# Gated linear attention with a routed expert layer: f loaded one chunk ahead of q, k and v, and the work that needs f alone done one step sooner

## Chip, cores, metric

One core of one Trainium2 chip. The metric is the time of one execution on the device in microseconds; a run is profiled once and timed in several rounds beside the kernel before.

## The reference, cut to what matters

A gated linear attention (batch 4, 8 heads, 768 positions, head size 48) feeds a layer of eight experts. The change touches the attention alone; the experts' routing and matrices (some 304 us of the span) are the same in both kernels.

```python
def _attn_ref(q, k, v, f_logit):
    f = 1.0 / (1.0 + np.exp(-f_logit))
    state = np.zeros((B, H, D, D))
    for t in range(S):
        state = f[:, :, t, :, None] * state + np.einsum('bhd,bhe->bhde', k[:, :, t], v[:, :, t])
        y[:, :, t] = np.einsum('bhd,bhde->bhe', q[:, :, t], state)
    return y
# then: assign each token to one of 8 experts by logits = x @ w_gate (384 tokens each),
# out = relu(x @ w1[e]) @ w2[e]
```

## The kernel before: the parts that matter

The attention runs in 24 chunks of 128 positions (4 batches x 6). A chunk passes through stages, and step s works on several chunks at once: a part listed with stage n works on chunk s - n. PE, VectorE (DVE), ScalarE (ACT) and GpSimd (POOL) keep the order of these lists; the loads on SyncE (SP) do not have to. The names: g is minus the logarithm of the forget factors, L its cumulative sum; dl is L within limits; eq and ek are its two exponentials; qg = q * eq and kg = k * ek; T is their transpose in PSUM, qT and kT the copies; A are the scores, am the masked ones; Y is the output in PSUM, x its copy, X and xT the transpose of x; R is the old state times its decay gl; "ends" are the sums from which gl comes.

```python
    def load(G):                      # four loads of 192 KB, rows of 192 bytes
        for nm, src in (("f", f_logit), ("q", q), ("k", k), ("v", v)):
            t = work.tile([128, H, DH], FP32, name=nm, tag=nm, bufs={"f": 3, "q": 4, "k": 4, "v": 7}[nm])
            nc.sync.dma_start(...)
    def clamp(G):  # POOL   f
    def decays(G): # ACT    f <- exp(-f), g <- ln(1 + f)
    def split(G):  # DVE upper <- g; POOL low <- g - upper     (chunks 2 and later)
    def split_high(G): # ACT high <- upper
    def sums(G):   # PE     L <- cumulative sums of g (two matmuls: high, low)
        if G["i"] == STAGES - 1:      # STAGES = 6
            idle_turns(3, ps("nothing", "sum"))
    def factors(G):# DVE dl <- L; ACT eq <- exp(-dl), ek <- exp(dl)
    def gated_q(G):# DVE    qg <- q * eq
    def gated_k(G):# POOL   kg <- k * ek
    def span(G):   # DVE spans <- ends; POOL gl; ACT gl
    def columns(G, nm, t):            # PE transposes qg, kg; 4 idle turns each for chunks 1, 2
    def queries(G):# PE Y += R qT; ACT x <- Y; store of x issued by ACT
    # ... transposed: PE X <- x; x_copy: DVE xT <- X; gate: PE; scores: PE A, DVE am; values: PE Y

    FIRST = ((decayed, 2), (q_columns, 2), (k_columns, 2), (transposed, 5), (sums, 1))
    FILLING = (FIRST + ((x_copy, 5), (factors, 1), (k_copy, 2), (added, 2), (values, 4), (halves, 1), (gate, 5),
                        (gated_q, 1), (new_state, 2), (decays, 0), (gated_k, 1), (span, 1), (to_logits, 5),
                        (split, 0), (beside, 0), (clamp, -1), (queries, 4), (split_high, 0), (scores, 3)))
    FULL = ((decayed, 2), (decays, 0), (transposed, 5), (sums, 1), (added, 2), (x_copy, 5), (factors, 1),
            (split, 0), (split_high, 0), (k_copy, 3), (halves, 1), (new_state, 2), (values, 4), (span, 1),
            (gate, 5), (gated_q, 1), (gated_k, 1), (to_logits, 5), (q_columns, 2), (k_columns, 2), ...,
            (beside, 0), (clamp, -1), (queries, 4), (scores, 3))
    # ... FILLING for steps 0 to 5, FULL to step 25, LAST to step 28;
    # `beside` holds small pieces of the routing, on VectorE and GpSimd

    constants()
    idle_turns(19, ps("nothing", "sum"))   # matmuls on constants that keep PE's clock up
    clamp(chunks[0])
    attention(0, 2)
    idle_turns(12, ps("nothing", "sum"))
    attention(2, 3)
    nc.vector.memset(a_bufs[2][:], 0.0)
```

Of the kernel before, what the change touches and what calls it, by code (L numbers as in the profile page):

```python
# [26 lines left out]
def kernel(  # L27
# [60 lines left out]
    def ps(name, tag="bank"):  # L88
        return banks.tile([128, 512], FP32, name=name, tag=tag, bufs=BANKS[tag])
# [34 lines left out]
    def idle_turns(n, nothing):  # L124

        for _ in range(n):
            nc.tensor.matmul(out=nothing[:, 0:CAP], lhsT=ones[:], rhs=idle[:], start=True,  # L127
                             stop=True)
# [28 lines left out]

    state, spare = {}, {}

    def load(G):  # L160
        b, c = G["b"], G["c"]
        for nm, src in (("f", f_logit), ("q", q), ("k", k), ("v", v)):

            t = work.tile([128, H, DH], FP32, name=nm, tag=nm,
                          bufs={"f": 3, "q": 4, "k": 4, "v": 7}[nm])
            nc.sync.dma_start(
                out=t[:], in_=src[b, :, C * c:C * c + C, :].rearrange("h t d -> t h d"))
            G[nm] = t

    def clamp(G):  # L170
        f = G["f"]
        nc.gpsimd.tensor_scalar(out=f[:], in0=f[:], scalar1=3.0e38, scalar2=-40.0,
                                op0=ALU.min, op1=ALU.max)
# [23 lines left out]

    def sums(G):
        g = g_bufs[G["i"] % NB]
        if G["i"] == STAGES - 1:  # L200

            idle_turns(3, ps("nothing", "sum"))
        G["L"] = L = ps("L")
        Lv = L[:, 0:D].rearrange("t (h d) -> t h d", d=DH)
        if "terms" in G:
            for n, term in enumerate(G["terms"]):
                nc.tensor.matmul(out=L[:, 0:D], lhsT=wcum_r[:],
                                 rhs=term[:].rearrange("t h d -> t (h d)"),
                                 start=(n == 0), stop=(n == 1))
        else:  # L210
            nc.tensor.matmul(out=Lv, lhsT=wcum[:], rhs=g[:, :, 0:DH], start=True, stop=True)
# [176 lines left out]
    chunks = [{"b": b, "c": c, "i": c * B + b} for c in range(NCH) for b in range(B)]  # L388
    AHEAD = 2
    STAGES = 6  # L390

    def beside(G):
# [6 lines left out]



    FIRST = ((decayed, 2), (q_columns, 2), (k_columns, 2), (transposed, 5), (sums, 1))
    FILLING = (FIRST + ((x_copy, 5), (factors, 1), (k_copy, 2),
                        (added, 2), (values, 4), (halves, 1), (gate, 5), (gated_q, 1),
                        (new_state, 2), (decays, 0), (gated_k, 1), (span, 1), (to_logits, 5),
                        (split, 0), (beside, 0), (clamp, -1), (queries, 4), (split_high, 0),
                        (scores, 3)))
    FULL = ((decayed, 2), (decays, 0), (transposed, 5), (sums, 1), (added, 2), (x_copy, 5),
            (factors, 1), (split, 0), (split_high, 0), (k_copy, 3), (halves, 1), (new_state, 2),
            (values, 4), (span, 1), (gate, 5), (gated_q, 1), (gated_k, 1), (to_logits, 5),  # L410
            (q_columns, 2), (k_columns, 2), (k_last, 2), (beside, 0), (clamp, -1), (queries, 4),
            (scores, 3))
    LAST = ((scores, 3),) + FIRST + ((x_copy, 5), (k_copy, 2), (values, 4), (queries, 4),
                                     (counts_so_far, 5), (gate, 5), (to_logits, 5),
# [3 lines left out]

    def attention(first, last):
        for step in range(first, last):  # L420
            if step + AHEAD < len(chunks):
                load(chunks[step + AHEAD])
            for part, stage in (FILLING if step < STAGES else
                                FULL if step < len(chunks) + 2 else LAST):
                if 0 <= step - stage < len(chunks):
                    part(chunks[step - stage])
                if part is sums and small_pe:
                    small_pe.popleft()()
                if part is beside:
                    for _ in range(min(len(small), 1 if step >= len(chunks) + 2 else 2)):  # L430
                        small.popleft()()

    for G in chunks[0:AHEAD]:
        load(G)
    nc.sync.dma_start(out=wg[:], in_=moe_w_gate.rearrange("(c p) e -> p c e", p=128))
    ENG = mybir.EngineType
    in_order = tc.manual_schedule(engines={ENG.PE, ENG.DVE, ENG.Activation, ENG.Pool})
# [1 line left out]
    constants()  # L439
    idle_turns(19, ps("nothing", "sum"))  # L440
    clamp(chunks[0])
    attention(0, 2)
    idle_turns(12, ps("nothing", "sum"))
    attention(2, 3)
    nc.vector.memset(a_bufs[2][:], 0.0)
    nc.scalar.dma_start(out=xd[N:N + 32, :], in_=zeros[:])
# [251 lines left out]
    def assign_and_run(begun=None, also=None, again=None, exact=None):  # L698
# [158 lines left out]
        def assign_exact(choice, over, pick, slots):  # L857
# [9 lines left out]
            n = E * NT  # L867
            sums = P[:, 0:n].rearrange("p (e c) -> p e c", c=NT)
            nc.tensor.matmul(out=sums, lhsT=ones[:], rhs=by_e(tie), start=True, stop=True)
            nc.tensor.matmul(out=P[:, n:2 * n], lhsT=after[:], rhs=by_e(tie), start=True, stop=True)  # L870
            sure = rt([NT, E], "sure", BF16)
# [285 lines left out]
        stack.close()  # L1157

    attention(3, ALL - 13)
    assert not small  # L1160
    begun, part, at_steps = begin()
# [109 lines left out]
    with tc.If(again[0] > 0):  # L1271
# [9 lines left out]
        with tc.For_i(0, B, 1) as b:  # L1281
# [7 lines left out]
            for c in range(NCH):  # L1289
                G = {"x": x[:, c, :]}  # L1290
# [42 lines left out]
```

## Time and profile before

| | before |
|---|---|
| time (median of 4) | 459.16 us (458.33 to 461.3) |
| profiled span | 457.7 us |
| first L (L(0)) starts | 6.86 us |
| L of step 6, of step 7, of step 23 | 30.80, 36.85, 129.79 us |
| last logits of the attention | 153.94 us |
| last logits to the end (routing and experts) | 303.8 us |

L(i), the cumulative sum of chunk i, is one matmul group a step, so its starts are a good clock. Before, step s has L(s-1); after the change, L(s). So one compares by step number. The page, the stretches and one step are shown in the prediction.

### The profile page before, as it was taken

What the parts mean: (1) busy time and instruction counts of PE and PEld (TensorE: products, weight loads), DVE (VectorE), ACT (ScalarE), POOL (GpSimd) and SP (SyncE); (2) the same over time, 40 slices, a digit from 0 to 9 for tenths busy, and PEclk for the clock granted to TensorE, in tenths of its full rate; (3) what the DMA queues carried; (4) which work ended last, traced back from release to release, by engine and by line L of the source; (5) the groups of instructions that cost most, each with busy time, mean ns of one, the idle gap of its engine ahead of it and who ended that gap; (6) DMA issues with size and microseconds to landing.
All of it is one profiled execution on the core that took longest, in us unless ns stands there. A gap on an engine that the chain in (4) does not pass through costs nothing. (4 is left out here: it accounts for less than half of the span.)

```text
span 457.7 us, 11902 instructions
## 1 busy us (share of the span) xinstructions
PE 437.1 (96%) x4893; PEld 293.8 (64%) x4893; DVE 266.0 (58%) x878; ACT 138.8 (30%) x322; POOL 135.6 (30%) x189
## 2 busy tenths in 40 slices
PE   8999999999999669999999999999999999999994
PEld 5788888888888535565565565565565565556552
DVE  5779986778987686657547547647637636000000
ACT  4566665565552001202202212212212212212210
POOL 1556655555551021032032033033023025101001
PEclk9999999999999859999999999999999999999998
DMA  9999988978611127082082082072082087400001
GB/s 158 186 196 196 201 177 190 202 166 189 141 37 39 36 86 245 1 310 70 8 299 74 8 292 80 3 290 82 6 292 70 17 292 243 174 19 34 0 19 39
DMA packets 118399, 59.11 MB, mean 129 GB/s; under 512 B 101664, under 2 KB 112960, under 8 KB 118336
## 3 DMA queue, kind: packets, MB, share of 16 engines
q1 hardware_dynamic: 111760, 44.06, 38.4%
q0 software_dynamic: 3072, 9.44, 6.3%
q10 hardware_dynamic: 3504, 4.77, 3.0%
q8 instruction: 40, 0.66, 0.6%
q14 instruction: 23, 0.19, 0.1%
HBM read 48.77 MB, written 9.49 MB: 127 GB/s over the span
## 5 line engine op out<-in xcount | busy, mean ns | idle before, releaser
L1054 PE MATMUL H<-xeT,w 128*128 128x384 f32 x384 | 132.6, 496 | 0.1
L1054 PEld LDWEIGHTS H<-xeT,w 128*128 128x128 f32 x384 | 69.1, 190 | 45.7 <-issue 4.0
L1066 PE MATMUL O<-w,hT 128*128 128x384 f32 x192 | 67.0, 491 | 0.0
L1066 PE MATMUL last_O<-w,hT 128*128 128x384 f32 x192 | 66.7, 491 | 0.0
L1058 ACT ACTIVATE hT<-H 128x384 f32<-128x384 f32 x64 | 31.4, 491 | 101.3 <-PE H L1054 85.3
L1066 PEld LDWEIGHTS last_O<-w,hT 128*128 128x128 f32 x192 | 35.1, 190 | 22.8 <-issue 1.9
L1066 PEld LDWEIGHTS O<-w,hT 128*128 128x128 f32 x192 | 34.9, 190 | 21.5 <-issue 1.3
L1071 POOL DMA_INDIRECT out_dram<-o,token x21 | 21.2, 1012 | 83.6 <-ACT o L1070 83.3
L324 DVE COPY_PREDICATED am<-mask,A 128x512 f32<-128x512 int32 x48 | 32.3, 726 | 14.9 <-PE A L319 14.9
L971 POOL TENSOR_TENSOR block<-past 128x72 f32<-128x72 f32 x8 | 2.4, 300 | 111.8 <-DVE at L551 100.1
L190 POOL TENSOR_TENSOR low<-g,upper 128x384 fp32r<-128x384 f32 x22 | 22.3, 1013 | 43.8 <-DVE upper L188 37.8
L1046 ACT COPY xeT<-Xe 128x384 f32<-128x384 f32 x24 | 11.4, 479 | 58.0 <-PE Xe L1043 57.7
L334 PE MATMUL Y<-v,am 128*64 128x48 f32 x768 | 27.6, 223 | 0.9 <-DVE am L324 0.9
L319 PE MATMUL A<-qT,kT 48*64 48x128 f32 x768 | 26.3, 272 | 0.0
L334 PEld LDWEIGHTS Y<-v,am 128*64 128x64 f32 x768 | 24.8, 138 | 1.9 <-DVE am L324 1.4
L1013 POOL DMA_INDIRECT xe<-xd,token x21 | 21.4, 1021 | 10.9 <-issue 4.3
L243 POOL TENSOR_TENSOR kg<-k,ek 128x384 f32<-128x384 f32 x23 | 23.1, 1004 | 2.4 <-ACT ek L221 2.4
L319 PEld LDWEIGHTS A<-qT,kT 48*64 48x64 f32 x768 | 21.2, 133 | 0.6 <-issue 0.6
L127 PE MATMUL nothing<-idle,ones 128*128 128x384 bf16 x74 | 19.8, 407 | 1.6 <-DVE ones L132 1.5
L220 ACT ACTIVATE eq<-dl 128x384 f32<-128x384 f32 x24 | 12.5, 522 | 24.7 <-DVE dl L218 24.7
L1070 ACT COPY o<-O 128x384 f32<-128x384 f32 x12 | 5.8, 479 | 40.7 <-PE O L1066 40.7
L237 DVE TENSOR_TENSOR qg<-q,eq 128x384 f32<-128x384 f32 x24 | 17.4, 725 | 0.6 <-ACT eq L220 0.6
(223 smaller groups left out, 659.7 us busy)
## 6 DMA issues: line engine op xcount, KB each, us to landing
w<-in_moe_w_dram SPq DMA_DIRECT2D x16, 1536.0 KB, 7.4
f<-in_f_logit_dram SPq DMA_DIRECT2D x24, 192.0 KB, 5.0
q<-in_q_dram SPq DMA_DIRECT2D x24, 192.0 KB, 4.8
k<-in_k_dram SPq DMA_DIRECT2D x24, 192.0 KB, 5.2
v<-in_v_dram SPq DMA_DIRECT2D x24, 192.0 KB, 5.2
xd<-x ACTq DMA_DIRECT2D x24, 192.0 KB, 3.4
xe<-xd,token POOLq DMA_INDIRECT x21, 3.1
out_dram<-o,token POOLq DMA_INDIRECT x21, 2.6
```

The costliest lines, as they stand in the source:

```text
L127: nc.tensor.matmul(out=nothing[:, 0:CAP], lhsT=ones[:], rhs=idle[:], start=True, stop=True)
L190: nc.gpsimd.tensor_tensor(out=low[:], in0=g[:, :, 0:DH], in1=upper[:].bitcast(FP32), op=ALU.subtract)
L237: nc.vector.tensor_tensor(out=G["qg"][:, :, 0:DH], in0=G["q"][:], in1=G["eq"][:], op=ALU.mult)
L243: engine.tensor_tensor(out=G["kg"][:, :, 0:DH], in0=G["k"][:], in1=G["ek"][:], op=ALU.mult)
L319: nc.tensor.matmul(out=A[par][HC * j:HC * j + HC, 128 * hp:128 * hp + 128], lhsT=G["kT"][rows, hp, HC * j:HC * j + HC], rhs=G["qT"][rows, ...
L324: nc.vector.copy_predicated(am[:, par], mask[:].unsqueeze(1).to_broadcast((128, HP, 128)), A[par][:].rearrange("s (a t) -> s a t", t=128))
L334: nc.tensor.matmul(out=Y[par][HC * j:HC * j + HC, DH * hp:DH * hp + DH], lhsT=G["am"][:, par, hp, HC * j:HC * j + HC], rhs=G["v"][:, 2 * h ...
L1013: nc.gpsimd.indirect_dma_start(out=xe[:], out_offset=None, in_=xd[:, :], in_offset=bass.IndirectOffsetOnAxis(ap=token[:, i:i + 1], axis=0))
L1054: nc.tensor.matmul(out=L["H"][:, 0:CAP], lhsT=L["w1"][:, d, 128 * ft:128 * ft + 128], rhs=xT[:, d, :], start=(d == 0), stop=(d == DC - 1))
L1058: nc.scalar.activation(out=hT[:, ft, :], in_=L["H"][:, 0:CAP], func=AF.Relu)
L1066: nc.tensor.matmul(out=L["O"][:, 0:D], lhsT=hT[:, ft, 128 * i:128 * i + 128], rhs=L["w2"][:, ft, :], start=(ft == 0), stop=(ft == FC - 1))
L1071: nc.gpsimd.indirect_dma_start(out=outs[next(tiles)][:, :], out_offset=bass.IndirectOffsetOnAxis(ap=L["token"][:, i:i + 1], axis=0), in_=o ...
```

## The change

Intent: f is the head of the longest chain (clamp, exp, ln, split, L, dl, eq, then qg). Load it earlier and do all of that chain one step sooner, so that q and k meet factors that have long been ready.

```diff
-    def load(G):
+    def load(G, names):
...
     def sums(G):
-        if G["i"] == STAGES - 1:
-            idle_turns(3, ps("nothing", "sum"))
...
-    FIRST = (... (sums, 1))
+    FIRST = (... (sums, 0))
     FILLING: (factors, 1) (halves, 1) (span, 1) -> 0;  (decays, 0) (split, 0) (split_high, 0) -> -1;  (clamp, -1) -> -2
              (gated_q, 1) and (gated_k, 1) move up, to stand right after (x_copy, 5), ahead of factors
     FULL:    the same stages, the same move of gated_q and gated_k
...
-            if step + AHEAD < len(chunks):
-                load(chunks[step + AHEAD])
+            for ahead, names in (AHEAD + 1, "f"), (AHEAD, "qkv"):
+                if AHEAD <= step + ahead < len(chunks) and (ahead == AHEAD or step >= 0):
+                    load(chunks[step + ahead], names)
...
-    for G in chunks[0:AHEAD]:
-        load(G)
+    for n, names in (0, "f"), (1, "f"), (0, "qk"), (2, "f"), (0, "v"), (1, "qkv"):
+        load(chunks[n], names)
...
-    attention(0, 2)
+    attention(-1, 2)
```

(The lines on the lists are told, not quoted.)

More of the change, by code (lines that the diff above doesn't have):

```diff
@@ L158 @@
     state, spare = {}, {}
-    def load(G):
+    def load(G, names):
         b, c = G["b"], G["c"]
-        for nm, src in (("f", f_logit), ("q", q), ("k", k), ("v", v)):
+        for nm in names:
+            src = {"f": f_logit, "q": q, "k": k, "v": v}[nm]
             t = work.tile([128, H, DH], FP32, name=nm, tag=nm,
@@ L395 @@
     ALL = len(chunks) + STAGES - 1
-    FIRST = ((decayed, 2), (q_columns, 2), (k_columns, 2), (transposed, 5), (sums, 1))
-    FILLING = (FIRST + ((x_copy, 5), (factors, 1), (k_copy, 2),
-                        (added, 2), (values, 4), (halves, 1), (gate, 5), (gated_q, 1),
-                        (new_state, 2), (decays, 0), (gated_k, 1), (span, 1), (to_logits, 5),
-                        (split, 0), (beside, 0), (clamp, -1), (queries, 4), (split_high, 0),
+    FIRST = ((decayed, 2), (q_columns, 2), (k_columns, 2), (transposed, 5), (sums, 0))
+    FILLING = (FIRST + ((x_copy, 5), (gated_q, 1), (gated_k, 1), (factors, 0), (k_copy, 2),
+                        (added, 2), (values, 4), (halves, 0), (gate, 5),
+                        (new_state, 2), (decays, -1), (span, 0), (to_logits, 5),
+                        (split, -1), (beside, 0), (clamp, -2), (queries, 4), (split_high, -1),
                         (scores, 3)))
-    FULL = ((decayed, 2), (decays, 0), (transposed, 5), (sums, 1), (added, 2), (x_copy, 5),
-            (factors, 1), (split, 0), (split_high, 0), (k_copy, 3), (halves, 1), (new_state, 2),
-            (values, 4), (span, 1), (gate, 5), (gated_q, 1), (gated_k, 1), (to_logits, 5),
-            (q_columns, 2), (k_columns, 2), (k_last, 2), (beside, 0), (clamp, -1), (queries, 4),
+    FULL = ((decayed, 2), (decays, -1), (transposed, 5), (sums, 0), (added, 2), (x_copy, 5),
+            (gated_q, 1), (gated_k, 1), (factors, 0), (split, -1), (split_high, -1), (k_copy, 3),
+            (halves, 0), (new_state, 2), (values, 4), (span, 0), (gate, 5), (to_logits, 5),
+            (q_columns, 2), (k_columns, 2), (k_last, 2), (beside, 0), (clamp, -2), (queries, 4),
             (scores, 3))
```

## The prediction

> **What bounds the kernel now.** I read the page first. The tenths by slice show where the change can act: the attention part, slices 1 to 13 (0 to about 150 us). After it comes the expert part, which this change does not touch.
>
> ```profile
> span 457.7 us, 11902 instructions
> PE   8999999999999669999999999999999999999994
> DMA  9999988978611127082082082072082087400001
> ```
>
> PE is busy and the DMA engines are nearly full up to about 120 us, so either could be the bound. The table of stretches separates them (columns: busy us of each engine with instruction counts, granted clock, DMA share, GB/s).
>
> ```profile
> 6.00:30.00 24.00, 23.50 (x396) 18.04 (x395) 16.20 (x40) 14.15 (x32) 10.81 (x16) 1.00 1.21 188
> 36.50:82.50 46.00, 44.96 (x1192) 40.04 (x1192) 37.48 (x93) 28.03 (x72) 27.44 (x41) 1.00 0.92 192
> 82.50:135.00 52.50, 52.08 (x1352) 45.84 (x1348) 45.51 (x115) 31.94 (x81) 30.31 (x46) 1.00 0.68 149
> ```
>
> Two regimes. In the filling (6 to 30 us) PE starts only 396 matmuls, against 1192 in the 46 us after, though it reads as busy: part of that time is idle turns that keep its clock up, the rest waits. From 36.5 us PE issues without a break.
>
> I took the steps one by one from the timeline, by the start of the three transposes X<-ident,x, of which each step has one group: 29.88, 36.55, 41.76, 47.43, 53.10, 58.78, 64.45, 70.12, 76.86 and so on to 135.03. The common period is 5.67 us; the mean from 36.55 to 135.03 is 98.48/17 = 5.79. A PE step has about 5.5 us of issue (queries 0.50, scores 1.00, X 0.30, L 0.53, dS 0.50, ends 0.46, Y 0.94, gate 0.42, two groups of transposes 1.02, start to start, and less than 0.2 of gaps). But PE is not alone. The chain of the other engines in one normal step, from the timeline (start, duration, engine, line, what):
>
> ```profile
> 64.57 1.35 DVE L324 COPY_PREDICATED am<-mask,A 128x512 f32<-128x512 int32 x2 [1.35 <-PE A L319]
> 65.82 0.54 DVE L369 COPY xT<-X 128x384 f32<-128x384 f32 x1
> 66.28 0.55 DVE L218 TENSOR_SCALAR dl<-L 128x384 f32<-128x384 f32 x1
> 66.88 0.36 DVE L188 TENSOR_SCALAR upper<-g 128x384 int32<-128x384 int32 x1
> 67.38 1.01 POOL L190 TENSOR_TENSOR low<-g,upper 128x384 fp32r<-128x384 f32 x1 [2.42 <-PE Y L334]
> 68.35 0.51 POOL L251 TENSOR_TENSOR gl<-spans 128x4 f32<-128x4 f32 x1
> 68.89 0.21 ACT L253 ACTIVATE gl<-gl 128x4 f32<-128x4 f32 x1 [0.69 <-POOL gl L251]
> 69.01 0.57 ACT L269 COPY qT<-T 128x512 f32<-128x512 f32 x1
> 69.47 0.54 ACT L355 COPY x<-Y 128x192 f32<-128x192 f32 x2
> 70.12 0.55 PE L363 MATMUL X<-ident,x 128*128 128x128 f32 x3
> ```
>
> Not data but order in the queues makes this a chain: gl stands behind low on GpSimd, qT and x stand behind gl on ScalarE. It ends when PE needs x for the next X, with hardly 0.1 us of slack. The next step proves that it has none: there ScalarE began its exp late (its queue stood at an earlier DMA issue), upper came late, and PE stood:
>
> ```profile
> 73.66 0.36 DVE L188 TENSOR_SCALAR upper<-g 128x384 int32<-128x384 int32 x1 [1.16 <-ACT g L178]
> 76.85 0.31 PEld L363 LDWEIGHTS X<-ident,x 128*128 128x128 f32 x3 [1.23 <-ACT x L355]
> ```
>
> A delay of 1.16 us at upper became a step of 6.74 instead of 5.67. So two things bound the steady steps at once: PE's own 5.5 to 5.6, and this chain.
>
> **What the Trainium skill says.** Perfetto Trace Analysis, section "Tensor Engine Instruction (MATMUL, LD_WEIGHTS)": ScalarE, VectorE and GpSimd are strict FIFO, so a new order in the program is a new order on the engine. The trace agrees: VectorE runs xT, dl, upper, kT, st, spans, qg, logits in every step, as FULL has them. GPSIMD Engine Reference, section "Specifications": GpSimd shares its SBUF interfaces with VectorE and contends with instructions there that have two SBUF inputs. The trace agrees: qg, with two such inputs, takes 551 ns at least, 718 in the median and 1310 at most, the long ones beside low, gl or kg. TensorE: Matmul & The Clock Gate, section "What's actually happening": the clock falls after an idle window of some 3.4 us. In this trace the granted clock is 1.00 in all of the attention steps.
>
> **The change, part by part.** Work: three idle matmuls are removed (326 ns each in the tile's view); nothing else is added or removed. They stood ahead of L(5), which waited for the high part anyway, so their worth is about 0.
>
> *Loads.* f(i) moves ahead by one chunk, and is needed one step sooner; q, k and v do not move. A step s needed f(s-1) for L, and needs f(s) now, which lies in the queue where f(s-1) did. No bytes change. I expect nothing of it in the steady part, where DMA has share 0.92 or less.
>
> *One stage more.* L(i) goes from step i+1 to step i, and columns, scores and outputs stay at i+2 and later. So step 0 now has work (L(0), ends(0)), and step 24 loses L and ends. What it costs depends on what sets the pace of the filling. There L goes 11.00, 15.34, 20.54, 25.64, 30.80: about 5.15 us apart, and the time between two of them is a ring. From 20.54: L done and dl 21.57, eq 22.16, then ek, exp of the next f 23.00, its ln, upper, low 24.67, L 25.64. It holds no wait for a load in this round. FILLING keeps decays behind factors, so the ring is the same after the change, only one step earlier in step numbers. L(0) stays at 6.86 (it stands behind 19 idle turns). L(1) need not wait for columns(0) and comes when g(1) is done (9.68 + 0.52), at 10.3 instead of 11.0. L(2) then comes at 14.8, behind the 12 idle turns and columns(0), and L(3) to L(6) at 20.0, 25.1, 30.3, 35.4. In step 6 this is L at 35.4 where the kernel before has L at 30.80: 4.6 late. The step from 6 to 7, 6.67 before by X with a wait of PE of 0.99 that began with exp(6) waiting on clamp and load, should be some 0.7 shorter. So at step 7 the change is behind by 4.6 - 0.7 = **+3.9 us** (3.0 to 4.7).
>
> *The new order in FULL.* qg comes ahead of dl and upper on VectorE: it takes some 0.46 from start to start (0.55 alone, with the overlap that xT to dl shows), and pushes dl, upper, low, gl, qT and x. kg goes to the front on GpSimd, where it was idle (low waits for upper 37.8 us in all), and is free. For qg, GpSimd's low and gl are no longer beside it, so it costs 0.55 instead of 0.72. The chain from am to X grows from 5.55 to about 6.0. It reaches from one step's am to the X of the next step but one group, so it makes a cycle of two steps with PE's own way from X to the next am (64.45 to 70.24, 5.79): before 11.34 for two; after, 11.34 + 0.46 - 0.12 slack = 11.68, 5.84 a step, +0.17. After about 100 us VectorE is itself near its limit (am at 124.16 had no wait for A), and there the 0.17 to 0.4 us that qg saves count against this. I take +0.1 a step for 16 steps, **+1.6 us**.
>
> *Draining.* Step 24 loses L (0.53) and ends (0.46) on PE, but waits for am there: **-0.8 us**.
>
> Sum: 459.2 + 3.9 + 1.6 - 0.8 = **463.9 us**.
>
> **The rivals.** First, *the f work is what holds the steps*, and with a step of slack PE runs at its own 5.5: 16 steps from 5.79 to 5.6 give -3.0, so 459.2 + 3.9 - 3.0 - 0.8 = 459.3. For it speak X's waits for x (8.0 us in 22 times over the run) and the 1.07 us lost in the step at 70.12; against it, that decays, dl, upper and low keep their places relative to each other within a step. Second, *the longer chain costs its full 0.46 in each step*, if kT, pushed too, holds up the scores of the same step: 16 x 0.46 = 7.4, and the time is 469.7. For it: kT ended at 67.83 and the transposes kg to T began at 68.09; against it, the scores that need kT start 1.3 us after its end. Third, *the loads pace the filling*: the share there is 1.21, and clamp waited for f in 6 cases. Then f a chunk sooner hides some of the ring's delay, the lag at step 7 is 2 instead of 3.9, and the time is 462.0.
>
> **Range and chances.** The sum of the terms' lower ends is about 459 and of their upper ends 468.5. To be faster by over 2% (below 450) would need the whole steady part at under 5.3 us a step, below PE's issue time: 0.02. Slower by over 2% (above 468.4) is the second rival nearly in full: 0.08. The rest, 0.90, is within 2%. Range 459 to 468.
>
> **What would show each step right or wrong.** Right: L(2) to L(6) still some 5.1 us apart, L in step 6 at 34.5 to 36; X to X in the steady part 5.7 to 5.9, with PE waiting for x before X more than now; qg at about 0.55 us; X in step 24 to the next X under 5.0 us; the expert part as long as before. Wrong: L in the filling at under 4.7 us apart, so that the stage costs nothing; a steady step under 5.67 without a wait at X; or a steady step over 6.0 with a wait at the scores for kT.

## The result, and the profile after

465.4 us (465.19 to 465.87, 4 runs) against 459.16: **slower, ratio 1.0128**, 95% interval 1.0096 to 1.0161. A ratio is the mean time of one kernel's runs over that of the other's of the same rounds, so it is not quite the ratio of the medians quoted. The time lies inside my range (459 to 468), and at 2% it counts as the same.

The 5.7 us of the profiled spans (463.4 - 457.7), cut at the L's:

| stretch | before | after | difference | predicted |
|---|---|---|---|---|
| start to L of step 7 | 36.85 | 43.41 | +6.56 | +3.9 |
| step 7 to step 23 | 92.94 | 92.22 | -0.72 | +1.6 |
| step 23 to the last logits | 24.15 | 23.91 | -0.24 | -0.8 |
| last logits to the end | 303.8 | 303.9 | +0.1 | 0 |

So the sum was nearly right, but two of its terms were not. First the page after, then its table of stretches (columns as in the prediction):

```profile
span 463.4 us, 11905 instructions
PE   6898999999998759999999999999999999999994
PEclk9989999999999857999999999999999999999998
```

```profile
6.00:30.00 24.00, 20.04 (x268) 14.51 (x270) 11.56 (x28) 12.09 (x26) 9.97 (x12) 0.93 1.25 182
82.50:135.00 52.50, 52.44 (x1412) 46.45 (x1404) 41.26 (x115) 32.36 (x85) 28.28 (x47) 1.00 0.67 145
```

In the third slice of PEclk stands an 8 that is not there before: from 6 to 30 us PE starts 268 matmuls instead of 396, and the mean granted clock is 0.93. In the late steady part VectorE is busy for 41.26 us instead of 45.51, with as many instructions.

The timeline after, in step 3 and 4 (start, duration, engine, line, what, and the idle time ahead):

```profile
18.78 2.25 POOL L191 TENSOR_TENSOR low<-g,upper 128x384 fp32r<-128x384 f32 x1 [2.06 <-DVE upper L189]
18.86 0.91 DVE L445 MEMSET am<- 128x1024 f32 x1 [0.16 <-DVE upper L189]
19.69 0.49 DVE L235 TENSOR_TENSOR qg<-q,eq 128x384 f32<-128x384 f32 x1
...
21.09 0.45 PE L205 MATMUL L<-low,wcum_r 128*128 128x384 f32 x1 [1.34 <-POOL low L191]
...
24.05 1.46 PE L127 MATMUL nothing<-idle,ones 128*128 128x384 bf16 x4
...
27.26 0.42 PE L205 MATMUL L<-high,wcum_r 128*128 128x384 f32 x1
```

low(3) takes 2.25 us instead of 1.01 while VectorE clears the third am buffer and then makes qg(2), which the new order has put there; PE waits for it 1.34 us between the two parts of L(3). Soon after, four idle matmuls take 1.46 us instead of 0.82: the clock has fallen. The stretches show the fall (the third number from the right is the granted clock):

```profile
20.00:22.00 2.00, 0.92 (x19) 0.73 (x21) 0.61 (x2) 0.00 (x0) 2.00 (x3) 1.00 0.80 157
22.00:24.00 2.00, 2.00 (x54) 1.69 (x49) 1.06 (x4) 1.81 (x4) 0.47 (x1) 0.73 1.04 202
24.00:26.00 2.00, 2.00 (x12) 1.36 (x9) 1.83 (x5) 0.58 (x2) 1.25 (x3) 0.50 1.13 198
26.00:28.00 2.00, 2.00 (x19) 1.43 (x18) 0.34 (x2) 0.59 (x1) 1.84 (x3) 0.92 1.35 203
```

L(3) to L(4) is 7.96 us for that, where all others from L(1) on are 4.4 to 5.7.

In the steady part, the chain that I had lengthened on paper by 0.46 us is longer by 0.13. An undisturbed step before, its first and last link, and then one after the change:

```profile
58.90 1.35 DVE L324 COPY_PREDICATED am<-mask,A 128x512 f32<-128x512 int32 x2 [0.52 <-PE A L319]
...
63.68 0.54 ACT L355 COPY x<-Y 128x192 f32<-128x192 f32 x2
```

```profile
83.67 1.36 DVE L322 COPY_PREDICATED am<-mask,A 128x512 f32<-128x512 int32 x2 [1.62 <-PE A L317]
...
85.40 0.53 DVE L235 TENSOR_TENSOR qg<-q,eq 128x384 f32<-128x384 f32 x1
85.86 0.54 DVE L216 TENSOR_SCALAR dl<-L 128x384 f32<-128x384 f32 x1
...
87.77 0.20 POOL L249 TENSOR_TENSOR gl<-spans 128x4 f32<-128x4 f32 x1
...
88.58 0.54 ACT L353 COPY x<-Y 128x192 f32<-128x192 f32 x2
```

From am to x it is 88.58 - 83.67 = 4.91 us; before it was 63.68 - 58.90 = 4.78, and 4.78 again in nearly all undisturbed steps of before and of e12 (below). qg now stands ahead of dl and costs its 0.46, but gl takes 0.20 us instead of 0.51, since qg is not beside it any more. There was slack for the rest: x was ready 0.23 us ahead of the next X in such steps of before, and is ready some 0.10 us ahead of it now. The step that the prediction quotes, with 4.90 from am to x and 0.11 ahead of X, is no undisturbed one: exp began late in it, and upper waited for g. An undisturbed step is 5.67 to 5.68 us in both kernels.

### The profile page after: what moved, and what is told of

Same layout as the page of the kernel before. It is cut to its first block, busy times and chain, and to the rows that moved or that the text cites. A ratio compares the mean times of both kernels' runs of the same rounds, so it can differ in the third digit from the quotient of the medians.

```text
span 463.4 us, 11905 instructions
## 1 busy us (share of the span) xinstructions
PE 439.1 (95%) x4890; PEld 294.6 (64%) x4890; DVE 257.5 (56%) x878; ACT 138.8 (30%) x322; POOL 131.3 (28%) x189
## 5 line engine op out<-in xcount | busy, mean ns | idle before, releaser
L191 POOL TENSOR_TENSOR low<-g,upper 128x384 fp32r<-128x384 f32 x22 | 23.7, 1078 | 54.8 <-DVE upper L189 29.8
L1070 ACT COPY o<-last_O 128x384 f32<-128x384 f32 x11 | 5.3, 479 | 40.5 <-PE last_O L1066 40.5
```

The lines of the kernel that those rows point to most:

```text
L191: nc.gpsimd.tensor_tensor(out=low[:], in0=g[:, :, 0:DH], in1=upper[:].bitcast(FP32), op=ALU.subtract)
```

## The experiments

Theory: of the lag at step 7, some 4 us are the added stage (one turn of the ring in the filling, that is, of the loop of waits that leads from one L to the next), and the rest is the fall of the clock, begun by a low(3) that was held up and by waits of PE that no idle matmuls fill. Rivals: the lag is the ring alone; the falls of the clock cost nothing; the steady part is set by the chain and the order; the loads set the pace.

All results in one table. "L(0) to step 7" and "7 to 23" are read from each run's profile by L; from L(0), since L(0) starts anywhere from 5.99 to 7.47 us, whatever the kernel. "Half clock" is the time at 0.5 between L(0) and the last logits. The rows come from different rounds, and before's median was 458.3 to 460.0 in them: compare rows by the ratios. A profile is one execution, and single steps of 5.9 to 7.3 us in some of them (below) move "7 to 23" by up to 2 us; "L(0) to step 7", too, is 28.65 to 30.52 in the four profiles with before's stages and order in the filling (before, e5, e10, e12).

| run | time, us | ratio to before (95%) | L(0) to step 7 | 7 to 23 | half clock |
|---|---|---|---|---|---|
| before | 459.16 | 1 | 29.99 | 92.94 | 0 |
| after | 465.4 | 1.0128 (1.0096 to 1.0161) | 36.69 | 92.22 | 3.4 |
| e1 after, memset early | 465.24 | 1.0102 (1.006 to 1.0144) | 38.84 | 91.42 | 13.7 |
| e2 after, idle turns in L(3) | 463.11 | 1.0085 (1.0031 to 1.014) | 35.85 | 91.12 | 3.4 |
| e3 after, old order | 469.34 | 1.0189 (1.0143 to 1.0236) | 36.80 | 93.80 | 6.8 |
| e4 after, an idle turn a step | 466.43 | 1.0165 (1.0103 to 1.0228) | 36.82 | 93.16 | 3.4 |
| e5 before, loads alone | 459.47 | 1.0011 (0.9987 to 1.0035) | 28.65 | 94.00 | 0 |
| e6 e5, exp first | 461.3 | 1.0054 (1.0027 to 1.0082) | 31.16 | 94.74 | 0 |
| e7 e1, exp first | 460.24 | 1.0046 (1.0023 to 1.007) | 30.47 | 92.82 | 0 |
| e8b e1, idle turns in all waits | 463.07 | 1.0085 (1.0063 to 1.0107) | 34.13 | 93.52 | 0 |
| e9 e7, store later | 460.46 | 1.004 (1.0023 to 1.0056) | 32.48 | 93.47 | 0 |
| e10 before, store later | 458.65 | 0.9999 (0.9982 to 1.0016) | 28.87 | 93.87 | 0 |
| e11 e7, store by SyncE | 459.16 | 1.0019 (0.9994 to 1.0044) | 30.27 | 91.55 | 0 |
| e12 before, store by SyncE | 457.96 | 0.9988 (0.9958 to 1.0017) | 30.52 | 91.93 | 0 |

**e1: the memset out of the way.**

```diff
         nc.vector.memset(zeros[:], 0.0)
+        nc.vector.memset(a_bufs[2][:], 0.0)
...
-    nc.vector.memset(a_bufs[2][:], 0.0)      # after step 2
```

> The kernel after, with the memset of the third a buffer moved from behind step 2 to the constants at the start, where VectorE is idle. Theory: of the 6.6 us by which L is late in step 7, some 4 are the added stage and the rest began when GpSimd's low(3) took 2.25 us instead of 1.0 beside this memset, which left PE idle for some 3 us in all and brought the granted clock to 0.5 for about 4 us. Then low(3) is back at 1.0 to 1.3 us, the low part of L(3) comes at about 19.9 instead of 21.1, the clock may stay at 1.0, and the time is 462.3 to 464.2. Rival: the whole lag is the stage (the ring sets the pace, the long low only fills a gap): time within 0.4 us of 465.4 and L(7) within 0.5 us of 43.4.

low(3) fell from 2.25 to 1.24 us, as expected. But the memset alone was not what held it up: in before, and in e3 below, where qg is back at its old place, the same memset runs beside a low that takes 1.01 us. The lines of e3:

```profile
18.43 1.01 POOL L191 TENSOR_TENSOR low<-g,upper 128x384 fp32r<-128x384 f32 x1 [2.05 <-DVE upper L189]
18.51 0.91 DVE L445 MEMSET am<- 128x1024 f32 x1 [0.16 <-DVE upper L189]
```

With qg alone beside it low takes 1.24 us (e1, e8b), with the memset and then qg 2.25 or 2.26 (after, e2, e4). So it was the two together, and the new order had its part in it. The time did not move (the intervals of the two ratios overlap): the clock fell elsewhere, twice, for 6.8 us each time. The stretches of e1:

```profile
10.00:12.00 2.00, 1.31 (x2) 0.50 (x2) 0.32 (x1) 0.60 (x2) 0.00 (x0) 0.62 1.39 173
...
38.00:40.00 2.00, 2.00 (x24) 1.56 (x24) 1.68 (x4) 1.14 (x3) 2.00 (x6) 0.50 1.03 249
```

The first fall follows a wait of PE that after, e2, e3 and e4 have too (2.02 us between ends(0) and L(1), where PE waits for g(1)); in the profiles of after, e3 and e4 the clock did not fall there. So which wait lets the clock fall differs from run to run, and taking away one of them proves nothing. The rival "the lag is the ring alone" is not refuted by this run either.

**e2: the wait filled.** The memset stays; eight idle matmuls go between the parts of L(3).

```diff
                                  start=(n == 0), stop=(n == 1))
+                if n == 0 and G["i"] == 3:
+                    idle_turns(8, ps("nothing", "sum"))
```

> The kernel after, with eight idle matmuls between the two parts of L(3), where PE waited 1.3 us for low(3). The memset stays, so low(3) stays at some 2.2 us. Theory: the half clock from 22 to 26 us costs time by itself, since PE is what step 3 and 4 wait for (columns(2), then L(4) at 27.3 though low(4) was there at 25.7); with the clock kept at 1.0, L(4) comes at 25.8 to 26.3 and the time is 463.9 to 464.5. Rival: the half clock falls into time that the ring gives away anyway: L(4) at 27.0 or later, time within 0.4 us of 465.4.

low(3) was 2.26 us, and the fall at 22 us was gone: L(4) came at 25.90, as the theory had it. But the profile has a fall of 3.4 us at 11.7 us, after the 2.02 us wait. Three of the four runs (462.85 to 463.35) lie below all of after's, and the fourth is 466.33; the intervals of the two ratios overlap. The mean granted clock of each run: 0.975 in the three, 0.969 in the fourth. It is the same in e4 below, 0.973 to 0.976 in three runs and 0.962 in the fourth, which is 4 us longer. So in both kernels the execution with by far the lowest clock is the slowest, which speaks against the rival that the falls cost nothing.

**e3: the old order with the new stages.**

```diff
-    FULL: ... (x_copy, 5), (gated_q, 1), (gated_k, 1), (factors, 0), ... (gate, 5), (to_logits, 5), ...
+    FULL: ... (x_copy, 5), (factors, 0), ... (gate, 5), (gated_q, 1), (gated_k, 1), (to_logits, 5), ...
     (FILLING likewise: both behind gate, as before)
```

> The kernel after with its stages and loads, but gated_q and gated_k back at their old places in the order of both lists. My prediction said that qg ahead of dl and upper lengthens the chain to x by 0.46 us and costs 0.1 us a step: then this run is 1.6 us faster than after (463.8), with steady steps shorter. Theory now, from the trace of after (undisturbed steps 5.67 to 5.68 as before): the order is not felt, because PE's own pass is 5.67 and because gl takes 0.20 us instead of 0.52 without qg beside it; then the time is within 0.6 us of 465.4 and gl is back at 0.5 us. A third way: the new order is what made the later steps shorter, and this run is 0.7 us or more slower.

The order of the prediction fell: putting qg back was not faster by 1.6 us but, in this profile, slower, 93.80 instead of 92.22 us in the steady part. gl is back at 0.51 us. Undisturbed steps stay at 5.67, so it is single steps that grow: the last eight of the steady part, which hold the small pieces of the routing, take 47.87 us instead of 46.10 (46.96 in before). This is no matter of one profile: they take 45.9 to 46.1 in six of the seven profiles with the new order and no idle turns added to these steps (46.9 in e8b), and 46.5 to 48.7 in all six with the old one. One such piece, in before and in after:

```profile
115.96 1.04 DVE L548 TENSOR_SCALAR steps<-count,step 128x16 f32<-128x16 f32 x1
```

```profile
122.37 0.25 DVE L548 TENSOR_SCALAR steps<-count,step 128x16 f32<-128x16 f32 x1
```

Before, kg runs on GpSimd beside these pieces, and the one shown ends when kg ends; after, it runs beside the last 0.22 us of low instead, and kg runs beside am and xT, which cost the same either way. Not all of e3's 469 us is this order: its profile has 6.8 us of half clock in step 6, and its expert part took 307.0 us instead of 303.9, with another 6.8 us of half clock there.

**e4: is PE the bound in the steady part?**

```diff
+        if G["i"] >= 7:
+            idle_turns(1, ps("nothing", "sum"))
         G["L"] = L = ps("L")
```

> The kernel after with one idle matmul (128x384 bf16, some 0.16 us of array time at full clock) ahead of each L from chunk 7 on, 17 in all. If PE's own pass is what bounds the steady steps, each is longer by 0.16: steps of 5.83 and a time longer by 2.2 to 3.0 us (467.6 to 468.4). If the chain over VectorE, GpSimd and ScalarE to x bounds them and PE has slack, the steps stay at 5.67 and the time stays within 0.7 us of 465.4.

Three L's of after, then of e4, from the timelines:

```profile
83.85 0.42 PE L205 MATMUL L<-high,wcum_r 128*128 128x384 f32 x1
89.53 0.42 PE L205 MATMUL L<-high,wcum_r 128*128 128x384 f32 x1
95.21 0.42 PE L205 MATMUL L<-high,wcum_r 128*128 128x384 f32 x1
```

```profile
83.62 0.48 PE L207 MATMUL L<-high,wcum_r 128*128 128x384 f32 x1
89.47 0.48 PE L207 MATMUL L<-high,wcum_r 128*128 128x384 f32 x1
95.31 0.48 PE L207 MATMUL L<-high,wcum_r 128*128 128x384 f32 x1
```

5.68 became 5.84, in nearly all steps: the 0.16 us of one matmul comes through in full. The idle turn stands between X and the next am; in the prediction's cycle of two steps it lies once, so that cycle would have passed on half of it. PE's own pass is the bound of an undisturbed step. The time grew by less than expected (the ratio by 0.0037, some 1.7 us, with intervals that overlap; 2.2 to 3.0 was expected): after had steps of 6.0 to 6.3 us in this stretch, and e4 had but one over 6.0.

**e5 and e6: the loads alone, and the ring cut without a stage.** e5 is before with the load order of the change and four f buffers; e6 also puts decays first in FILLING.

```diff
     e5:  load(G, names) and its calls as in the change; bufs={"f": 4, ...}; stages as before
     e6:  e5, and
-    FILLING = (FIRST + (... (new_state, 2), (decays, 0), (gated_k, 1), ...
+    FILLING = (((decays, 0),) + FIRST + (... (new_state, 2), (gated_k, 1), ...
```

> The kernel before with the loads of the change alone: f one chunk ahead of q, k and v, in the same order of issue, with four f buffers instead of three; stages and order as before. Theory: the loads do not set the pace (ring in the filling, PE's pass after), so nothing moves: time within 1 us of before's 460.0 in these rounds, L(5) at 30.3 to 31. Rival: the loads pace the filling; then clamp no longer waits for f, L(5) comes at 29.5 or earlier, and the run is 1.5 us or more faster than before.

> As e5_loads_alone, and in the filling exp and ln of the next f go ahead of the factors on ScalarE, as they do in the full steps; no stage is added. Theory: the ring (L, dl, eq, ek, exp of the next f, ln, upper, low, next L; 5.15 us) is what paces the filling, and this cuts it, since exp no longer stands behind eq and ek; L(1) to L(5) are then 4.2 to 4.6 us apart, L(5) comes at 27 to 29 instead of 30.8, and the time is 1.5 to 3.5 us under before, if the granted clock stays at 1.0. Rival: q, k, v or PE pace the filling as closely as the ring does; then L(5) stays at 30 or later and the time within 1 us of before.

e5: level, within 0.35%, L(5) at 30.51. Loading f ahead is worth nothing by itself. e6 is my miss: L(5) came at 31.97, later than before (25.93 us after L(0) instead of 23.94), and the run is 0.5% slower. With exp first a new ring closes, over GpSimd: kg waits for ek, clamp of the next f stands behind kg and low, exp waits for clamp, and now eq and ek stand behind exp. In its trace it goes kg 23.71, low 25.06, clamp 26.05, exp 26.59, ln 27.14, qT 27.57, eq 28.04, ek 28.46, kg 29.05: 5.34 us, as long as the one that was cut.

**e7: the ring cut with the added stage.** e1, with decays first in FILLING.

```diff
-    FILLING = (FIRST + (... (new_state, 2), (decays, -1), (span, 0), ...
+    FILLING = (((decays, -1),) + FIRST + (... (new_state, 2), (span, 0), ...
```

> The kernel after, with the memset moved to the start, and exp and ln of the next f ahead of the factors in the filling as well. Theory: the lag of the added stage is one turn of the ring, so cutting the ring takes most of it away: L(6) at 30 to 33 instead of 37.8, and a time of 457 to 460 if the clock stays at 1.0 (some 2.5 us more for each fall of the clock). Rival: the stage costs a whole step of PE work and waits whatever the ring does: L(6) at 35 or later and a time of 462 or more.

Here kg needs an ek of the step before, so no such ring closes. Step 7 comes 30.47 us after L(0), 6.2 us sooner than in after, and no time of the filling is at half clock, with no added idle turns. The time is 460.24; by the ratios (1.0046 and 1.0128) it is some 3.8 us under after's, clear of the intervals. So the added stage costs little here (30.47 us to step 7, against 28.65 to 30.52 in the profiles with before's filling): its price in after was mostly the ring's turn. L(1) shows where the turn went; the timelines of e7 and of e8b (below):

```profile
7.18 0.81 PE L210 MATMUL L<-g,wcum 128*128 128x384 f32 x2
8.48 0.91 PE L210 MATMUL L<-g,wcum 128*128 128x384 f32 x2
```

```profile
7.03 0.81 PE L214 MATMUL L<-g,wcum 128*128 128x384 f32 x2
10.42 0.91 PE L214 MATMUL L<-g,wcum 128*128 128x384 f32 x2 [0.29 <-ACT g L180]
```

L(1) follows L(0) after 1.30 us instead of 3.39, since g(1) is not made behind eq(0) and ek(0). From L(3) on the L's are 5.0 to 5.1 us apart all the same: there clamp waits for f to land (4.9 us in 4 waits from 15 to 44 us). So the loads seem to stand right behind the ring, and a filling much faster than before's is not to be expected from f; no run here loads f still sooner.

**e8b: the clock kept, the ring kept.** e1 with idle turns in all waits of the filling.

```diff
+        if G["i"] in (1, STAGES):
+            idle_turns(10 if G["i"] == 1 else 3, ps("nothing", "sum"))      # ahead of L(1), L(6)
...
+                if n == 0 and G["i"] == 3:
+                    idle_turns(4, ps("nothing", "sum"))                     # inside L(3)
...
+        if G.get("i") == 1:
+            idle_turns(4, ps("nothing", "sum"))                             # ahead of X in step 6
```

> The kernel after, with the memset moved to the start and idle matmuls in the waits of the filling: ten ahead of L(1), four between the parts of L(3), four ahead of X in step 6, three ahead of L(6) (as many as the change took away in that step); the ring stays. Theory: with no fall of the clock what is left of the lag is the added stage, one turn of the ring: granted clock 1.00 from 8 to 48 us, L(7) at 40.5 to 42 instead of 43.4, 3.9 to 5.2 us after before's L of the same step, and a time some 3 us over before. Rival: the falls of the clock cost nothing by themselves: L(7) at 43 or later and 465.

Its stretch, against the first one quoted of after:

```profile
6.00:30.00 24.00, 23.09 (x318) 16.71 (x316) 13.66 (x35) 13.61 (x31) 10.44 (x15) 1.00 1.23 184
```

The clock is 1.00 throughout. From L(0) to step 7 it takes 34.13 us: 4.14 more than before, 2.56 less than after. This is the run that splits the lag: **4.1 us for the added stage, 2.6 us for the clock and the held-up low together.** The 2.6 us lie in one place: L(3) to L(4) is 5.38 us here and 7.96 in after. In e2, with the held-up low but no fall there, it is 6.34, so about 1.0 us is the low and 1.6 the clock. The 4.1 is less sure: against the other profiles with before's filling (28.65 to 30.52) it is 3.6 to 5.5. The time, 463.07, is 0.85% over before's, and the granted clock of its four runs is 0.974 to 0.980, as in before's of the same rounds (after's: 0.968 to 0.970).

**e9 to e12: the long single steps.** My prediction quoted a step of 6.74 us in before, in which ScalarE began exp late. The timeline of e7 has the same thing (ACTq is ScalarE's queue issuing a DMA):

```profile
65.42 0.54 ACT L354 COPY x<-Y 128x192 f32<-128x192 f32 x2
67.89 0.34 ACTq L357 DMA_DIRECT2D xd<-x  x1
68.28 0.52 ACT L179 ACTIVATE f<-f 128x384 f32<-128x384 f32 x1 [2.31 <-DMA f<-in_f_logit_dram]
```

x was ready at 65.96, but ScalarE issued its store only at 67.89, when a load had landed, and everything behind it on that engine stood. The packed trace says which load: the program hands eight completion semaphores round its DMAs, and ahead of each issue the engine waits for the semaphore that this issue will use. This store's was last used by a load of f that was issued at 63.10 and landed at 67.81. In before's long step it is again a load of f (landed 72.08, store issued 72.16). e9 (on e7) and e10 (on before) issue the store one step later, behind high of the next step; e11 and e12 let SyncE issue it.

```diff
     e9, e10:  the dma_start of queries becomes a part of its own, (stored, 5), behind split_high in FULL
     e11, e12:
-        nc.scalar.dma_start(out=xd[row:row + C, :], in_=x[:])
+        nc.sync.dma_start(out=xd[row:row + C, :], in_=x[:])
```

> As e7_after_decays_first (which was 0.5% over before), and in the full steps ScalarE issues the store of x one step later, behind exp, ln, the factors and high of the next step. Theory: what still lengthens single steps in the steady part (5.8 to 6.2 us at 60 to 85 us) is that ScalarE's queue stands at this issue for up to 2.5 us, until an earlier load lands, with exp of f behind it; with exp ahead of it these steps are 5.67 to 5.7, the mean of steps 7 to 23 falls from 5.80 to 5.70 to 5.74 and the time is 1 to 1.6 us under e7's, level with before or just under it. Rival: the loads themselves are what those steps wait for, and the mean stays at 5.78 or more.

> The kernel before with the same later store of x alone. My prediction took the step of 6.74 us at 70 us (upper 1.16 us late, X waiting 1.23 us) for a delay of exp behind a DMA issue. If that is so, the 6.7 us step is gone, no step but those with much small work on VectorE is over 5.9, and the run is 0.8 to 1.5 us faster than before. If the lateness had another cause, the long step stays and the time is within 0.5 us.

> As e7_after_decays_first, with the store of x issued by SyncE instead of ScalarE, behind its loads. The store's issue on ScalarE stood until an earlier load had landed (up to 2.5 us), and putting it later on ScalarE only moved the stand (e9, e10). If ScalarE's stand is what lengthens the steps at 60 to 85 us, they are 5.67 to 5.7 now, the mean of steps 7 to 23 is 5.70 to 5.75, and the time is 1 to 1.5 us under e7's (459 or less), level with before. Rival: SyncE now stands at the store with the loads behind it, or the loads themselves are the bound; then single steps of 6 us and more stay or grow, and the time is e7's or worse.

> The kernel before with its stores of x issued by SyncE. The first theory of e11 says the 6.7 us step is gone and the run is 0.5 to 1.5 us faster than before; the rival says level or slower.

e9 and e10 failed: the store still had to wait (to 78.43 in e9, though its x was ready at 72.7: its semaphore was that of a load of k which landed at 78.41), now with gl, qT and x behind it, and steps of 7.27 and 6.96 us appeared. e11 and e12 show that the stand on ScalarE was the cause: in the steady part no step of 6 us is left but those at 105 to 130 us with much small work, and it takes 91.55 and 91.93 us, one profile each. In this undisturbed form the two orders differ by 0.4 us in 16 steps. The times hardly gain by it: 459.16 and 457.96 against 458.42 in the same rounds, both level within their intervals. No version was shown to beat the kernel before.

## Why the prediction was right, point by point

- *The loads, 0*: right. e5 does them alone: ratio 1.0011.
- *The added stage, +3.9 us at step 7*: right in mechanism, and in size as far as it can be told. L(1) and L(2) came at 10.11 and 14.55 (I had 10.3 and 14.8); e8b, with the clock kept, has +4.14 (3.6 to 5.5 against the other profiles with before's filling). My check "L(2) to L(6) still some 5.1 us apart" failed in after at one place alone, L(3) to L(4), 7.96 us.
- *"The granted clock is 1.00 in all of the attention steps"*: true of before and silently carried over to after, and that was the failed step in this term. In the kernel before idle turns stand at its own waits, and the clock stays at 1.00; the new stages make other waits (2.02 us ahead of L(1), 1.34 us in L(3), and 0.64 and 0.37 us ahead of X and L(6) in step 6, where three idle turns were taken out). That, with low(3) at 2.25 us, is +2.6 us. The prediction charged the new order to FULL alone; in FILLING it put a qg behind the memset, beside low(3), and the two together held it up.
- *"Their worth is about 0"* (the three idle turns): not settled alone. In the profile of after the clock did not fall at that place; in e1 and e3, without these turns as well, it did, for 6.8 us each. e8b, which has three turns there again among others, has no fall.
- *The new order in FULL, +1.6 us*: wrong in sign. Two parts of it failed. The chain did not grow by 0.46 but by 0.13: 4.91 us from am to x against 4.78 in undisturbed steps, since gl shrank from 0.51 to 0.20; I had credited qg with the freed contention, but not gl, which stood in the same chain. And the slack was 0.23 us to the next X, not 0.11: the "normal step" of the prediction had a late exp in it. And PE's pass is 5.67, not 5.5 (my own terms, 0.50 + 1.00 + 0.30 + 0.53 + 0.50 + 0.46 + 0.94 + 0.42 + 1.02, add up to 5.67), so PE was the bound, which e4 shows. What the order did change is small VectorE work that no longer runs beside kg; with the old order the steady part is 1.6 us longer (e3, one profile), and in e11 against e12 0.4 us. That kg is the reason is read from lines such as those under e3; no run moved kg alone.
- *The 6.74 us step as proof of the chain*: half right. A late exp does reach X through that chain; e12, with the store off ScalarE, has no such step. But it showed what a delay beyond the slack does, not that there was no slack.
- *Range*: its upper end can't be rebuilt from the terms: with 4.7 for the stage and the second rival in full they give 470.5, not 468.5. And a time below 450 with the stage's +3.9 asks for steps of 5.0 us, not 5.3.
- *Draining, -0.8 us*: right in sign, -0.24 measured. Step 24 lost L and ends, and PE waited for am there.
- *The third rival*, that the loads pace the filling: not so in after, where the ring does; but e7 suggests that they stand right behind it, at 5.0 us a chunk.

The total came out near because the clock's +2.6 and the order's -2.3 (-0.7 instead of +1.6) nearly cancel. That is luck, not skill.

## What to carry to other kernels

Working one stage sooner costs one more step of filling, and it pays only if the steady steps wait for that stage; here they were PE's own 5.67 us, so there was nothing to win. Matmuls on constants that keep the clock up are placed for one schedule: whoever moves work has to look for the new waits of PE and move them too. And before charging an instruction to a chain because it now stands in front of it, look at what it stood beside until now, and whether that is in the chain too.

## What the Trainium skill lacked or had wrong

- TensorE: Matmul & The Clock Gate, section "What's actually happening", has the clock fall after one idle window of some 3.4 us, and the table of its section "Why this matters for your kernels" allows gaps up to some 3 us. As rules for a kernel these two are too lenient; the page's section "A second HAM failure mode: psum-queue depth-cycling" has falls under frequent short idles, but gives no length. In these runs the clock fell with no gap near 3 us: after a longest gap of 2.02 us (e1, e2), after one of 1.34 us in a stretch where PE was busy for 2.44 of 4 us (after), and after gaps of 0.65 and 0.39 us (e1 at 37 us). The page's free-running window agrees: the half clock lasted 3.4 or 6.8 us in the fillings, once or twice the window, and the same 2.02 us wait brought a fall in e1 and e2 but none in after, e3 and e4.
- GPSIMD Engine Reference, section "Specifications", names the VectorE instructions that contend with GpSimd, those with two SBUF inputs among them. These runs agree and give sizes: gl 0.51 us beside qg and mostly 0.20 without; low 1.24 us beside qg and 1.01 without. I found no page with the case that cost most: a memset beside low costs nothing (1.01 us, in before and e3), but a memset with a qg behind it made low 2.25 us (after). Why is not settled by these runs.
- I found no page that warns that the issue of a store can stand on a compute engine's queue until a load lands whose data it does not touch, with that engine's work behind it: 1.9 us in the step of e7 quoted above, and gone from ScalarE with the store on SyncE (e11, e12). The reason is in the program, not in the chip: the two DMAs share one of its eight completion semaphores.
